# A fused attention and feed-forward kernel on one core: g's cast in batch index 1 from VectorE to ScalarE, the forms' steps over two slots, P's blocks of batch index 2 in pairs, and its score steps moved

## The chip, the cores and the metric

The kernel runs on one core of a Trainium2 chip. A core has a matrix engine (TensorE, PE in the profile; its weight loads are PEld), a vector engine (VectorE, DVE), an activation engine (ScalarE, ACT), GpSimd (POOL) and SyncE (SP), which here issues nearly all DMAs. Each engine runs its own instructions in the order in which they stand; semaphores order the engines among each other. The metric is the device time of one execution in microseconds, the median of several runs.

## The reference

Eight batches of eight heads: a slot attention (softmax over 32 memory slots, then over the scores) is followed by a feed-forward layer with SiLU. All is float32.

```python
def _attn_ref(q, k, v, phi):                 # q, k, v: 8 x 8 x 576 x 64; phi: 8 x 8 x 576 x 32
    a = np.exp(phi - np.max(phi, axis=2, keepdims=True))
    a = a / (np.sum(a, axis=2, keepdims=True) + 1e-09)
    k_m = np.einsum('bhsm,bhsd->bhmd', a, k)
    v_m = np.einsum('bhsm,bhsd->bhmd', a, v)
    scores = scale * np.matmul(q, k_m.transpose(0, 1, 3, 2))
    scores = scores - np.max(scores, axis=-1, keepdims=True)
    attn = np.exp(scores)
    attn = attn / (np.sum(attn, axis=-1, keepdims=True) + 1e-09)
    return np.matmul(attn, v_m)
def _moe_ref(x, w_in, w_out):                # x: 4608 x 512; w_in: 512 x 2048; w_out: 2048 x 512
    h = x @ w_in
    g = h * (1.0 / (1.0 + np.exp(-h)))
    return g @ w_out
```

## The kernel before

**What is multiplied.** The attention's last product and the first feed-forward product are taken together: per batch the kernel forms P = v_m · w_in (tiles `pm`), and h = attn · P. Every float32 factor is kept as a high part (a cast to fp32r, a copy) and a low part (the factor minus its high part), and a product is three matmuls: high·high, high·low, low·high. So each g = silu(h) needs a cast and a subtraction, and so do P (`p_split`: ACT casts at L677, DVE subtracts at L679) and the attention weights (`s_high` on ACT at L472, `s_low` on DVE at L479).

**Slots.** The work of a batch runs in 16 slots. Batch indices 0 and 1 take one block of 128 columns of the 2048 per slot. In a slot of batch index 1, PE does 12 matmuls for `h` (L701), then side work that a table of events puts there, then the 12 matmuls of `acc` (L746) for g of the slot before. In between ACT takes silu of h (L728, into `gbuf`; the 64 left-over columns into `gleft` at L730) and DVE casts g (L718) and takes the low part (L720), both into `gparts`, which holds two such pairs in turn. `h` is one PSUM tile, so the next h waits until ACT has read it. After slot 15 of an odd batch come four steps for the left-over tokens of two batches (`accleft` in batch index 1, `lsum` later; called steps 16 to 19 here, NFC = 16). From batch index 2 on, the second product is done with seven products in place of eight (`forms`, `st_step`, L854 and L893), whose weights `kept` and `saved` are derived from w_out by `w_forms` during batch index 1: eight pieces j, each with a step 0 (five DVE instructions, L814 to L821) and a step 1 (ACT casts at L835, DVE subtractions at L836, a DMA of 256 KB to `forms`).

**Side work for the next batch.** While batch b runs, the attention of batch b + 1 is made: `phi_max`, `phi_fold`, `phi_sub` (DVE), `phi_exp` (ACT), `e_mm` (PE, then DVE and ACT into `kvn`), `e_tr`, `s_all` (scores on PE, transposed by DVE), `s_max`, `s_sub` (L426, L430, DVE), `s_exp` (L434, ACT; the switch to the exponential's table and back is an ACT_TABLE_LOAD each), `s_sum` (L438 to L440), `s_norm` (L444), `s_back` (L464), `s_high`, `s_low`. P's four blocks of 512 columns (`p_mm`, L649) need w_in's blocks, which `win_load` brings back from HBM (1 MB each). `p_mm` with `beside` puts its result into two tiles of the pool `acc` (`pacc`), so that a second block need not wait for the tile `bg`.

**What sets the order.** `ev(b, slot, fn, ...)` enters a step into the table; the main loop runs the entries of a slot after that slot's h and silu. PE and ACT run in the order in which the code records their work. DVE's and SP's order is left to a scheduler, bounded by `behind(i, other)`, which puts an instruction after another on the same engine; `last_split[-1]` is the last subtraction of g's low part. In batch index 1 the scheduler is free to put `s_max` to `s_low` ahead of the slot's own split. POOL has nothing to do here.

Of the kernel before, what the change touches and what calls it, by code (L numbers as in the profile page):

```python
# [25 lines left out]
NFC = DFF // P  # L26
CW = 256
JW = 512
# [20 lines left out]
def attn_ffn_kernel(  # L49
# [756 lines left out]
    def w_forms(j, step):  # L806


        if step == 0:
            while len(kept) < 3 * j + 3:  # L810
                keep(*homes_left.pop(0))
            f = at[0]["forms", j] = sb.tile([P, 2, DMODEL], F32, tag="cva", name="wf", bufs=1)
            c = slice(2 * j, 2 * j + 2)
            i = nc.vector.tensor_tensor(f, as_f32(wo_hi[:, c]), as_f32(wo_lo[:, c]), op=ALU.add)  # L814
            if j == 0:
                behind(i.ins, last_split[-1])
            b11, b12, b21, b22 = (f[:, k, q * Q : (q + 1) * Q] for k in range(2) for q in range(2))
            nc.vector.tensor_tensor(b11, b12, b11, op=ALU.subtract)
            nc.vector.tensor_tensor(b12, b22, b12, op=ALU.add)
            nc.vector.tensor_tensor(b22, b22, b11, op=ALU.add)  # L820
            nc.vector.tensor_tensor(b21, b22, b21, op=ALU.subtract)  # L821
            return
        f = at[0]["forms", j].rearrange("p k (q f) -> p (k q) f", q=2)
        t1 = sb.tile([P, 1, DMODEL], F32R, tag="cva1", name="t1", bufs=1)
        runs = [[t1, 0, 1]]
        for u in range(3 * j, 3 * j + 3):
            t, i = kept_at[u]
            if t is runs[-1][0]:
                runs[-1][2] = i + 1
            else:  # L830
                runs.append([t, i, i + 1])
        n = 0
        for t, i, e in runs:
            src, to = f[:, n : n + e - i], t[:, i:e]
            nc.scalar.activation(to[:, :, :Q], src, AF.Copy)  # L835
            nc.vector.tensor_tensor(to[:, :, Q:], src, to[:, :, :Q], op=ALU.subtract)  # L836
            n += e - i
        load(saved[j], as_f32(t1[:, 0]))
# [182 lines left out]
    def steady(b, n):  # L1021


        early = b > 2
        if not early:
            ev(b, 1, phi_max, n)
            for i in range(3):
                ev(b, 2, phi_fold, n, i)
            ev(b, 3, phi_sub, n)
        ex = exp_slots(b)[0]  # L1030
        em = ex + 1 + b % 2
        ev(b, ex, phi_exp, n)
        ev(b, em, e_mm, n)
        for hf in range(2):
            ev(b, em + 1, load_q, n, hf)
        ev(b, ex + 4, e_tr, n)
        ev(b, ex + 5, s_all, n)
        ev(b, 9 if early else 10, s_max, n, ALL)
        ev(b, 10, s_sub, n, ALL)
        ev(b, 11, s_exp, n, ALL)  # L1040
        ev(b, 12 if early else 11, s_sum, n, ALL)
        ev(b, 13 if early else 12, s_norm, n, FIRST)
        turn = NFC + 3 if b % 2 else 14 if early else 13
        ev(b, turn, s_back, n, FIRST)
        ev(b, turn, s_high, n, FIRST)
        ev(b, turn, s_low, n, FIRST)
        for k in range(3):
            ev(b, 10 + 2 * k, win_load, n, k)
        if b % 2:
            ev(b, NFC, win_load, n, 3)  # L1050
        for k in range(2):
            ev(b, NFC + 2 if b % 2 else 13 + k, p_mm, n, k * JW, JW, True, b % 2 and k)
        m = n + 1
        if m < B:
            ev(b, ex + 3, load_kv, m, range(2))
            ev(b, ex + 3, load_phi, m)
            ev(b, ex + 6, load_kv, m, range(2, FULLC))
            ev(b, 7 if early else 14, phi_max, m)
            for i in range(3):
                ev(*((b, 11 + i) if early else (b + i // 2, (14, 15, 0)[i])), phi_fold, m, i, load)  # L1060
            ev(b + 1, 1, phi_sub, m)

    for b in range(B):
        n = b + 1
        if b == 0:
            for j in range(2, DFF // CW):
                ev(b, 2 * j - 1.5, p_mm, b, j * CW, CW)
        elif b == 1:
            ev(b, 0, win_save)
            for j in range(1, NJ):  # L1070
                ev(b, 4 * j - 3, p_mm, b, j * JW, JW)
            for j in range(NP):
                ev(b, 1.5 * j + 2, w_forms, j, 0)
                ev(b, 1.5 * j + 2.5, w_forms, j, 1)
        else:
            pair = b > 2 and b % 2 == 0
            if not pair:
                ev(b, 0, win_load, b, 3)
            ev(b, 0 if b > 2 else 1, p_mm, b, 2 * JW, JW)
            if b > 2:  # L1080
                ev(b, 3, s_norm, b, SECOND)
                for fn in (s_back, s_high, s_low):
                    ev(b, 4 + b % 2, fn, b, SECOND)
            late = b % 2 and 2 < b < B - 1
            ev(b, 0 if pair else 4 if late else 2, p_mm, b, 3 * JW, JW, not late, pair)
            if n < B:
                steady(b, n)
            if late:
                ev(b, 4, p_rest, b, 3 * JW)
            continue  # L1090
        at_slot = (
            (4, 5, 6, 7.5, 9, 9.5, 11.5, 12.5, 13, 13.5, 14, 14) if b == 0
            else (1, 2, 3, 5, 9, 10, 10, 11, 12, 13, 13, 14)
        )
        mx, sub, ex, em, tr, s0, s1, sx, se, ss, sn, sk = at_slot
        ev(b, mx, phi_max, n)
        if n == 1:
            ev(b, sub, phi_allmax, n, (0, 1), (0,))
            ev(b, sub + 0.5, phi_allmax, n, (0, 1), (1,))
        else:  # L1100
            for i in range(3):
                ev(b, sub, phi_fold, n, i)
        ev(b, sub + 0.5, phi_sub, n)
        ev(b, ex, phi_exp, n)
        ev(b, em, e_mm, n)
        ev(b, 14 if b == 0 else em + 1, load_kv, n + 1, range(FULLC if b == 0 else 2))
        ev(b, tr, e_tr, n)
        ev(b, em, load_q, n, 1)
        if n == 1:
            ev(b, s0, s_mm, n, 0)  # L1110
            ev(b, s1, s_mm, n, 1)
        else:
            ev(b, s0, s_all, n)
        if b == 0:
            ev(b, s1, load_q, n + 1, 0)
        else:
            ev(b, s1 + 1, load_kv, n + 1, range(2, FULLC))
        ev(b, sx, s_max, n, ALL)
        ev(b, sx, s_sub, n, ALL)
        ev(b, se, s_exp, n, ALL)  # L1120
        ev(b, ss, s_sum, n, ALL)
        ev(b, sn, s_norm, n, ALL)
        for u in (FIRST, SECOND) if n == 1 else (ALL,):
            ev(b, sk, s_back, n, ALL, u)
            ev(b, sk, s_high, n, ALL, u)
        ev(b, sk, s_low, n, ALL)
        ev(b, sk, load_phi, n + 1)
        if b == 0:
            ev(b, 14, p_mm, n, 0, JW)
        else:  # L1130
            for k in range(3):
                ev(b, 12 if k == 2 else 6 + k, win_load, n, k)
            for k in range(2):
                ev(b, 12 + 2 * k, p_mm, n, k * JW, JW)
    slots = [1.5, 1.5] + [2 * j - 1 if k == "i" else min(2 * j - 0.5, 12.5) for k, i in later for j in [i - 1 if k == "i" else i]]
    to_do = list(slots)
    for slot in slots:
# [151 lines left out]
    for b in range(B):  # L1289
# [10 lines left out]
        for fc in range(NFC if b < 2 else 0):  # L1300
# [3 lines left out]
                        fn(*a)  # L1304
                continue
            h = ffn1(b, fc, low_last=b == 1 and fc == 0)
            gs = split(silu(b, fc, h))
            for part in range(2):
                if b == 0:
                    finish((2 * part, 2 * part + 1))  # L1310
                traced = nc.cur_bb.bb.instructions
                n = len(traced)
                late = set()
                for fn, a in events.pop((b, fc + part / 2), []):
                    m = len(nc.cur_bb.bb.instructions)
                    fn(*a)
                    if fn is phi_max:
                        late.update(i.name for i in list(nc.cur_bb.bb.instructions)[m:])
                if b == 0:
                    for i in list(nc.cur_bb.bb.instructions)[n:]:  # L1320
                        if i.engine == ACT:
                            behind(i, last_silu[-1])
                        elif i.engine == DVE and (fc > 10 or i.name in late):
                            behind(i, last_split[-1])
            if b:
                finish(range(NI))
            prev = ("main", b, fc, gs)
        if b % 2:
            for n in range(NLS):
                gs = left_split(b, n)  # L1330
                if b > 1:
                    run(b, NFC + n)
                finish((0, 1, 2, 3))
                prev = ("left", b, n, gs)
    finish((0,))
# [55 lines left out]
```

## Time and profile before

| | us |
|---|---|
| median of 3 runs | 678.78 (678.55 to 679.08) |
| the profiled execution | 678.47 |
| its span, first to last instruction | 676.7 |
| what lies around the span (678.47 - 676.7) | 1.8 |
| mean granted clock | 0.999 |

A stretch in the views runs from the start of one block of matmuls on PE to the start of the next: batch index 1 from 105.66 (h of slot 0) to 189.35 us, its left-over steps to 197.52, batch index 2 to 272.77. Matmuls of one engine overlap in the records, so a block's own length is read from start to start, not from its busy time. On DVE and ACT an instruction's start can lie a little ahead of the end of the one before it, as the instructions are pipelined. The page's longest groups of PE are h of batches 2 to 7 (L854, 168.7 us in 1152 matmuls) and the seven products (L893). The trace shows the matmuls of all stages at the full clock.

### The profile page before, as it was taken

The numbers are of one execution on the slowest core, as the hardware profiler recorded it, in microseconds if no ns is written. First come the engines' busy times: TensorE is split into PE (matmuls) and PEld (weight loads), VectorE is DVE, ScalarE is ACT, GpSimd is POOL, SyncE is SP. The second block draws the span as 40 slices with busy tenths as digits, with TensorE's granted clock in tenths as the row PEclk, the third lists the DMA queues.
The fourth block names the chain that finished last, engine by engine and source line by source line (L and its number), as shares of the span: only waits on it lengthen the run. The fifth ranks groups of instructions, "written<-read, shape, count | busy, mean of one in ns | idle before, by whom it ended". The sixth has DMA issues, their size and how long they took to land.

```text
span 676.7 us, 14541 instructions
## 1 busy us (share of the span) xinstructions
PE 667.1 (99%) x5792; PEld 588.6 (87%) x5792; DVE 518.6 (77%) x1093; ACT 368.5 (54%) x681; POOL 0.7 (0%) x6
## 2 busy tenths in 40 slices
PE   7999999999999999999999999999999999999997
PEld 3577778787888998999988999899997999889996
DVE  4997899988948689868877688877877668867653
ACT  3878684533625556654655546564654546554541
POOL 0000000000000000000000000000000000000000
PEclk9999999999999999999999999999999999999999
DMA  9998975224270552253420535116430204300001
GB/s 340 373 339 276 315 304 192 81 103 146 78 233 22 184 183 100 79 180 124 179 95 16 185 97 179 70 42 237 157 126 32 86 2 156 111 31 17 32 1 47
DMA packets 37907, 93.92 MB, mean 139 GB/s; under 512 B 4688, under 2 KB 21456, under 8 KB 34256
## 3 DMA queue, kind: packets, MB, share of 16 engines
q1 hardware_dynamic: 36816, 90.22, 38.4%
q10 hardware_dynamic: 1024, 2.77, 1.1%
q8 instruction: 46, 0.75, 0.5%
q14 instruction: 21, 0.17, 0.1%
HBM read 77.22 MB, written 15.73 MB: 137 GB/s over the span
## 4 chain that ended last, share of the span: by engine, by line
PE 73%; DVE 10%; issue 2%; ACT 2%; DVEq 0%; ACTq 0%
PE sum L893 35%; PE h L854 22%; PE lsum L977 5%; PE bg L649 3%; PE acc L746 3%; PE h L701 2%; PE accleft L746 2%; DVE gparts L720 1%; PE bg L335 1%; PE bg L382 1%; DVE pm L679 1%; DVE kept L836 1%; DVE gparts L718 1%; DVE smx L426 1%; PE h L335 1%
## 5 line engine op out<-in xcount | busy, mean ns | idle before, releaser
L854 PE MATMUL h<-aparts,pm 128*128 128x288 f32 x1152 | 168.7, 295 | 0.0
L854 PEld LDWEIGHTS h<-aparts,pm 128*128 128x128 f32 x1152 | 157.3, 188 | 0.8
L868 ACT ACTIVATE gbuf<-h 128x512 f32<-128x512 f32 x96 | 57.3, 597 | 117.0 <-PE h L854 113.7
L893 PE MATMUL sum<-wo_hi,aparts 128*128 128x256 f32 x384 | 102.6, 289 | 0.0
L893 PE MATMUL sum<-kept,aparts 128*128 128x256 f32 x576 | 100.1, 282 | 0.0
L893 PE MATMUL sum<-wo_lo,aparts 128*128 128x256 f32 x384 | 100.0, 282 | 0.0
L873 DVE TENSOR_TENSOR gbuf<-gbuf 128x256 f32<-128x256 f32 x96 | 40.5, 422 | 71.4 <-ACT gbuf L868 70.9
L882 ACT ACTIVATE aparts<-gbuf 128x512 fp32r<-128x512 f32 x86 | 54.4, 633 | 63.4 <-DVE gbuf L877 63.4
L746 PE MATMUL acc<-wo_hi,gparts 128*128 128x512 f32 x256 | 85.0, 397 | 0.2
L893 PEld LDWEIGHTS sum<-wo_hi,aparts 128*128 128x128 f32 x384 | 72.8, 189 | 11.5 <-ACT gleft L870 10.1
L893 PEld LDWEIGHTS sum<-kept,aparts 128*128 128x128 f32 x576 | 82.6, 191 | 0.0
L884 DVE TENSOR_TENSOR gparts<-gbuf,aparts 128x512 fp32r<-128x512 f32 x86 | 59.5, 692 | 19.1 <-ACT aparts L882 19.1
L893 PE MATMUL sum<-wo_hi,gparts 128*128 128x256 f32 x384 | 73.2, 281 | 0.0
L893 PEld LDWEIGHTS sum<-wo_lo,aparts 128*128 128x128 f32 x384 | 73.1, 190 | 0.0
L893 PE MATMUL sum<-kept,gparts 128*128 128x256 f32 x288 | 65.5, 282 | 0.0
L746 PEld LDWEIGHTS acc<-wo_hi,gparts 128*128 128x128 f32 x256 | 47.6, 188 | 14.5 <-DVE gparts L720 1.5
L893 PEld LDWEIGHTS sum<-wo_hi,gparts 128*128 128x128 f32 x384 | 59.4, 190 | 0.0
L701 PEld LDWEIGHTS h<-aparts,pm 128*128 128x128 f32 x372 | 51.7, 188 | 6.8 <-issue 3.4
L701 PE MATMUL h<-aparts,pm 128*128 128x288 f32 x372 | 56.0, 299 | 0.6 <-DVE aparts L612 0.5
L872 ACT ACTIVATE aparts<-gbuf 128x384 fp32r<-128x384 f32 x96 | 50.4, 525 | 0.0
L746 PE MATMUL acc<-wo_lo,gparts 128*128 128x512 f32 x128 | 49.3, 393 | 0.4 <-DVE wo_lo L182 0.4
L893 PEld LDWEIGHTS sum<-kept,gparts 128*128 128x128 f32 x288 | 47.9, 190 | 0.0
(225 smaller groups left out, 956.1 us busy)
## 6 DMA issues: line engine op xcount, KB each, us to landing
win<-win_saved SPq DMA_DIRECT2D x24, 1024.0 KB, 5.2
kv<-in_kv SPq DMA_DIRECT2D x28, 516.0 KB, 5.0
q<-in_q SPq DMA_DIRECT2D x16, 576.0 KB, 6.2
raw<-in_w_in SPq DMA_DIRECT2D x14, 512.0 KB, 7.6
raw<-in_w_out SPq DMA_DIRECT2D x6, 1024.0 KB, 6.5
win_saved<-win SPq DMA_DIRECT2D x4, 1024.0 KB, 8.6
phi<-in_phi SPq DMA_DIRECT2D x7, 576.0 KB, 8.3
out<-oo SPq DMA_DIRECT2D x26, 128.0 KB, 2.3
```

The costliest lines, as they stand in the source:

```text
L335: nc.tensor.matmul(pt[p][M * r : M * (r + 1), :KVW], e[:, p, c, M * r : M * (r + 1)], kvt[c][:, p, r], start=c == 0, stop=False, skip_grou ...
L649: nc.tensor.matmul((bg[p][M * r : M * (r + 1)] if beside else bg[M * r : M * (r + 1), p, :w]).rearrange("p (k f) -> p k f", f=P), kvT[D * ...
L701: nc.tensor.matmul(h[:, hf, :HALF], wt[:, p, fs], a[:, p, hf * HALF : (hf + 1) * HALF], start=n[hf] == 0, stop=n[hf] == 5, skip_group_chec ...
L746: nc.tensor.matmul(acc[key], gt[:, cs], wt[:, fc], start=fc == 0 and n == 0, stop=fc == NFC - 1 and n == 2)
L854: nc.tensor.matmul(h[:, i, :HALF], wt[:, p, f : f + P], a[:, p], start=n == 0, stop=n == 5)
L868: nc.scalar.activation(gbuf[:, :MAIN].rearrange("p (i f) -> p i f", i=2), h[:, :, :w], AF.Silu)
L872: nc.scalar.activation(hi[:, :3], g[:, 1:4], AF.Copy)
L873: nc.vector.tensor_tensor(g[:, 4:6], g[:, :1].broadcast_to([P, 2, P]), g[:, 1:3], op=ALU.subtract)
L882: nc.scalar.activation(hi[:, 3:], g[:, 4:], AF.Copy)
L884: last_split.append(nc.vector.tensor_tensor(lo[:, 3:], g[:, 4:], hi[:, 3:], op=ALU.subtract))
L893: nc.tensor.matmul(sums[bank][:, place * Q : (place + 1) * Q], gt[:, k], wt, start=bank not in begun, stop=True, skip_group_check=True,)
L977: nc.tensor.matmul(sums[k], part[gt][:, 2 * i + k], wt[:, fc], start=n == 0 and i == 0 and m == 0, stop=True, skip_group_check=True,)
```

## The change

It has two parts. In batch index 1, g is cast by ACT (L716 in the new kernel, step 2 of `split`) in all slots but 3 and 12, those in which ACT takes an exponential; so is the last slot of batch index 0. The forms' pieces get a table of slots, with a step 1 about two slots behind step 0 or less; pieces 1 and 2 are held behind a split and behind the subtraction into `kvn`. `phi_max` and the score steps on DVE are held behind the split of their slot. The first two blocks of P for batch index 2 go from slots 12 and 14 into step 18, the second beside the first; w_in's fourth block is loaded in step 16. In batch index 2, P's third and fourth block go into slot 0 as a pair, `e_tr` from slot 8 to 7, `s_all` from 9 to 8, `s_max` from 10 to 9, `s_norm` from 12 to 13, `s_back` to `s_low` from 13 to 14, P's first block for the next batch from 13 to 12, `phi_max` from 14 to 12, and the folds of the maxima from slots 14, 15 and 0 into 13, 14 and 15. Lines below L1033 shift by up to 6 in the new kernel.

```diff
@@ w_forms
-            if j == 0:
-                behind(i.ins, last_split[-1])
+            if j < 3:
+                behind(i.ins, last_kvn[0] if j == 2 else last_split[-1])
@@ steady(b, n)
-        ev(b, ex + 4, e_tr, n)
-        ev(b, ex + 5, s_all, n)
-        ev(b, 9 if early else 10, s_max, n, ALL)
+        ev(b, ex + 4 - (not early), e_tr, n)
+        ev(b, ex + 5 - (not early), s_all, n)
+        ev(b, 9, s_max, n, ALL)
...
-        ev(b, 13 if early else 12, s_norm, n, FIRST)
-        turn = NFC + 3 if b % 2 else 14 if early else 13
+        ev(b, 13, s_norm, n, FIRST)
+        turn = NFC + 3 if b % 2 else 14
...
-            ev(b, NFC + 2 if b % 2 else 13 + k, p_mm, n, k * JW, JW, True, b % 2 and k)
+            ev(b, NFC + 2 if b % 2 else (13 if early else 12 + k) + k, p_mm, n, k * JW, JW, True, b % 2 and k)
...
-            ev(b, 7 if early else 14, phi_max, m)
+            ev(b, 7 if early else 12, phi_max, m)
             for i in range(3):
-                ev(*((b, 11 + i) if early else (b + i // 2, (14, 15, 0)[i])), phi_fold, m, i, load)
+                ev(b, 11 + i if early else 13 + i, phi_fold, m, i, load)
@@ the table
+    FORM_SLOTS = (2, 4), (4, 5), (5.5, 6.5), (7, 8), (8.5, 9.5), (10, 11), (11.5, 13), (13, 14)
-            for j in range(NP):
-                ev(b, 1.5 * j + 2, w_forms, j, 0)
-                ev(b, 1.5 * j + 2.5, w_forms, j, 1)
+            for j, (slot, end) in enumerate(FORM_SLOTS):
+                if j:
+                    ev(b, FORM_SLOTS[j - 1][1], w_forms, j - 1, 1)
+                ev(b, slot, w_forms, j, 0)
+            ev(b, end, w_forms, j, 1)
         else:
-            pair = b > 2 and b % 2 == 0
+            pair = b % 2 == 0
             if not pair:
                 ev(b, 0, win_load, b, 3)
-            ev(b, 0 if b > 2 else 1, p_mm, b, 2 * JW, JW)
+            ev(b, 0, p_mm, b, 2 * JW, JW)
...
-            for k in range(3):
-                ev(b, 12 if k == 2 else 6 + k, win_load, n, k)
+            for k, slot in enumerate((6, 7, 12, NFC)):
+                ev(b, slot, win_load, n, k)
             for k in range(2):
-                ev(b, 12 + 2 * k, p_mm, n, k * JW, JW)
+                ev(b, NFC + 2, p_mm, n, k * JW, JW, True, k)
@@ the main loop
-            gs = split(silu(b, fc, h))
+            by_act = fc not in (3, 12) if b else fc == NFC - 1
+            gs = split(silu(b, fc, h), steps=(2, 1) if by_act else (0, 1))
...
-                    if fn is phi_max:
+                    if fn is phi_max or b and fn in (s_max, s_sub, s_sum, s_norm, s_back, s_low):
                         late.update(i.name for i in list(nc.cur_bb.bb.instructions)[m:])
...
+                for i in list(nc.cur_bb.bb.instructions)[n:] if b else ():
+                    if i.engine == DVE and i.name in late:
+                        behind(i, last_split[-1])
...
             for n in range(NLS):
                 gs = left_split(b, n)
-                if b > 1:
-                    run(b, NFC + n)
+                run(b, NFC + n)
```

Where the instructions go, at three places. First ACT in slots 13 to 15 of batch index 1, from the first form cast of a piece (`t`) on. Before:

```order
L835 ACTIVATE t_1861<-wf 128x256
L835 ACTIVATE kept<-wf 128x3x256
L728 ACTIVATE gbuf<-h 128x512
L730 ACTIVATE gleft<-h 128x64
L472 ACTIVATE aparts<-aT_1901 128x1152
L677 ACTIVATE pm<-bg 128x1024
L728 ACTIVATE gbuf<-h 128x512
```

and now:

```order
L728 ACTIVATE gbuf<-h 128x512
L730 ACTIVATE gleft<-h 128x64
L716 ACTIVATE gparts<-gbuf 128x512
L835 ACTIVATE t_1883<-wf 128x256
L835 ACTIVATE kept<-wf 128x3x256
L472 ACTIVATE aparts<-aT_1889 128x1152
L728 ACTIVATE gbuf<-h 128x512
L730 ACTIVATE gleft<-h 128x64
L716 ACTIVATE gparts<-gbuf 128x512
```

The last piece's casts stood in slot 13 and now stand in slot 14; `s_high` (L472) stands in slot 14 in both, ahead of the silu of slot 15, and the cast of P behind it is gone. Each silu is now followed by its cast.

Second DVE, in slots 13 to 15 of batch index 1. Before, from `s_sum` to the split of slot 15:

```order
L440 RECIPROCAL ssm<-ssm 128x36
L821 TENSOR_TENSOR wf<-wf 128x256
L444 TENSOR_TENSOR sc_1701<-sc_1701,ssm 128x1152
L718 CAST gparts<-gbuf 128x512
L836 TENSOR_TENSOR t_1861<-wf,t_1861 128x256
L720 TENSOR_TENSOR gparts<-gbuf,gparts 128x512
L836 TENSOR_TENSOR kept<-wf,kept 128x3x256
L464 STREAM_TRANSPOSE aT_1901<-sc_1701 128x576
L718 CAST gparts<-gbuf 128x512
L464 STREAM_TRANSPOSE aT_1901<-sc_1701 128x576
L720 TENSOR_TENSOR gparts<-gbuf,gparts 128x512
L479 TENSOR_TENSOR aparts<-aT_1901,aparts 128x1152
```

and now, from the split of slot 14 to that of slot 15:

```order
L720 TENSOR_TENSOR gparts<-gbuf,gparts 128x512
L818 TENSOR_TENSOR wf<-wf 128x256
L440 RECIPROCAL ssm<-ssm 128x36
L819 TENSOR_TENSOR wf<-wf 128x256
L444 TENSOR_TENSOR sc_1693<-sc_1693,ssm 128x1152
L820 TENSOR_TENSOR wf<-wf 128x256
L836 TENSOR_TENSOR t_1883<-wf,t_1883 128x256
L821 TENSOR_TENSOR wf<-wf 128x256
L464 STREAM_TRANSPOSE aT_1889<-sc_1693 128x576 x2
L836 TENSOR_TENSOR kept<-wf,kept 128x3x256
L718 CAST gparts<-gleft 128x512
L479 TENSOR_TENSOR aparts<-aT_1889,aparts 128x1152
```

(the next row is L720, the split of slot 15). `s_norm` (L444) stood ahead of the split of slot 14 and stands behind it now; the transposes (L464) stand behind all of the last form; and the first left-over cast (L718 from `gleft`) and `s_low` (L479) stand ahead of the split of slot 15.

Third PE, in the left-over steps 17 and 18, now (three more alternations of the two `pacc` tiles follow):

```order
L746 MATMUL accleft<-wo_lo,gparts 128x512
L746 MATMUL accleft<-wo_hi,gparts 128x512
L649 MATMUL bg<-win_0_1513,kvT_1644 32x512 x8
L649 MATMUL pacc_1997<-win_1_1558,kvT_1644 32x512
L649 MATMUL pacc_1998<-win_1_1558,kvT_1644 32x512
```

Before, the two blocks (one each in slots 12 and 14) stood between a slot's h and its acc; this is slot 14 in the difference:

```order
 L746 MATMUL acc_1250<-wo_hi,gparts 128x512
 L701 MATMUL h<-aparts,pm 128x288 x12
-L649 MATMUL bg<-win_1_1564,kvT_1652 32x512 x8
 L746 MATMUL acc_1238<-wo_hi,gparts 128x512
 L746 MATMUL acc_1238<-wo_lo,gparts 128x512
```

So 16 matmuls a block left the slots, and 32 came in between the first and the second group of `accleft`.

## The prediction

> **What bounds the kernel now.** I read the page's head first, then the busy time by stage, from start to start of PE's blocks (columns: stretch, length, then busy us and instructions of PE, PEld, DVE, ACT, POOL, the granted clock, DMA share and GB/s).
>
> ```profile
> span 676.7 us, 14541 instructions
> PE 667.1 (99%) x5792; PEld 588.6 (87%) x5792; DVE 518.6 (77%) x1093; ACT 368.5 (54%) x681; POOL 0.7 (0%) x6
> ```
>
> ```profile
> 105.66:189.35 83.69, 83.35 (x607) 67.30 (x607) 74.36 (x146) 38.63 (x74) 0.00 (x0) 1.00 0.37 132
> 189.35:197.52 8.17, 8.17 (x37) 6.76 (x36) 2.21 (x4) 0.72 (x2) 0.00 (x0) 1.00 0.83 274
> 197.52:272.77 75.25, 75.12 (x715) 69.03 (x713) 58.27 (x133) 40.51 (x77) 0.00 (x0) 1.00 0.38 124
> 357.61:432.00 74.39, 74.39 (x715) 69.07 (x714) 57.50 (x130) 41.27 (x80) 0.00 (x0) 1.00 0.34 114
> ```
>
> PE sets the time everywhere. In batch index 1 (first row) DVE is nearly as full, 74.36 of 83.69 us; ACT has 38.63. So what the change can win are PE's waits there, and what it can lose is a DVE chain that comes late. PE's waits in this batch, from the view of waits between 100 and 200 us (total, times, longest), and five groups of `acc` from start to start:
>
> ```profile
> PEld acc L746 <- DVE gparts L720: 1.5, 3, 0.5
> ...
> PEld h L701 <- DVE kvn L361: 0.5, 1, 0.5
> ```
>
> ```profile
> 107.35:110.50 3.15, 3.08 (x12) 2.01 (x12) 1.70 (x3) 1.00 0.20 74
> 126.33:129.47 3.14, 3.04 (x12) 1.99 (x12) 0.00 (x0) 1.00 0.00 0
> 134.44:137.57 3.13, 3.02 (x12) 2.18 (x12) 0.00 (x0) 1.00 0.92 342
> 173.63:176.38 2.75, 2.75 (x12) 2.07 (x12) 0.00 (x0) 1.00 0.03 6
> 183.53:189.35 5.82, 5.75 (x24) 4.24 (x24) 1.67 (x3) 1.00 0.77 277
> ```
>
> Twelve undisturbed matmuls take 2.75 us (fourth row). The first two rows lose 0.40 and 0.39 to a late g; the third loses 0.26 (side work ahead of a group costs 0.12 by itself, below) to `kvn`; the last, two groups, 0.32. That is 1.4 us, all that waits could give in batch index 1.
>
> **P's blocks.** The rows are h, a block of P, acc and the next h around slot 12, and a pair in batch index 4:
>
> ```profile
> 166.47:168.15 1.68, 1.68 (x13) 1.51 (x11) 1.68 (x3) 0.00 (x0) 0.00 (x0) 1.00 0.85 346
> 168.15:169.17 1.02, 1.02 (x17) 0.18 (x16) 1.02 (x3) 0.25 (x1) 0.00 (x0) 1.00 0.07 24
> 169.17:172.04 2.87, 2.87 (x20) 2.36 (x13) 2.51 (x6) 2.84 (x6) 0.00 (x0) 1.00 0.25 97
> 172.04:173.63 1.59, 1.59 (x14) 1.58 (x12) 1.59 (x4) 1.59 (x2) 0.00 (x0) 1.00 0.00 0
> 359.28:361.16 1.88, 1.88 (x33) 0.49 (x33) 1.07 (x4) 1.18 (x4) 0.00 (x0) 1.00 0.04 9
> ```
>
> A single block costs 1.02, and 0.09 and 0.12 at its edges (1.68 against 1.59, 2.87 against 2.75): 1.23. A pair costs 1.88 and the same edges: 2.09. So slots 12 and 14 lose **-2.46**, step 18 gains **+2.09**. Batch index 2 gains 0.37 by its pair; its stretch is also 0.86 longer than batch 4's, which has this arrangement already, so between -0.37 and -0.86, and I take **-0.6**.
>
> **The cast.** DVE loses 14 casts of batch index 1 and one of batch 0, 0.42 each (a row below). ACT's cast of g is not in this stage; the nearest row is the same copy out of `gbuf` in later batches:
>
> ```profile
> L882 ACT ACTIVATE aparts<-gbuf 128x512 fp32r<-128x512 f32 x86 | 54.4, 633 | 63.4 <-DVE gbuf L877 63.4
> ```
>
> 0.63, with 0.42 (were it as fast as DVE) as the other end; ACT's spare 45 us hide it as long as nothing long stands ahead of it. The waits at 107.35 and 126.33 go: the cast no longer queues on DVE behind `s_low` or a form's sum, **-0.79**. What is late next at 134.44 is `kvn`. PE would be there at 137.57 - 0.26 - 0.79 = 136.5. In slot 5, h ends at 129.47 + 1.68 - 0.79 = 130.4; 0.16 of hand-over, silu 0.60 and cast 0.63 make 131.8. DVE then has the split (0.60), seven rows of 0.34 to 1.14 up to the last `kept` (0.34, 0.34, 1.14, four times 0.34) and four tiny ones for `rs` (0.4): 136.0. The rows below give 0.7 of waiting for ACT's half of `kvn` and 0.35: 137.1. PE waits 0.6 where it waited 0.26, **+0.34**. At slot 11 the gain is 0.45.
>
> ```profile
> L361 DVE TENSOR_SCALAR kvn<-h,rs 128x128 f32<-128x128 f32 x1 | 0.4, 351 | 0.7 <-ACT kvn L359 0.7
> ```
>
> **The end of batch index 1** decides. The rows of DVE and ACT in slots 12 to 15 of before (start, duration):
>
> ```profile
> 170.19 0.42 DVE L836 TENSOR_TENSOR kept<-wf,kept 128x256 fp32r<-128x256 f32 x1
> 170.53 0.42 DVE L718 CAST gparts<-gbuf 128x512 fp32r<-128x512 f32 x1
> 170.86 1.22 DVE L814 TENSOR_TENSOR wf<-wo_hi,wo_lo 128x1024 f32<-128x1024 f32 x1
> 172.00 0.69 DVE L720 TENSOR_TENSOR gparts<-gbuf,gparts 128x512 fp32r<-128x512 f32 x1
> 172.60 0.42 DVE L818 TENSOR_TENSOR wf<-wf 128x256 f32<-128x256 f32 x1
> 172.97 1.35 DVE L438 TENSOR_REDUCE ssm<-sc 128x36 f32<-128x1152 f32 x1
> 174.24 1.22 DVE L679 TENSOR_TENSOR pm<-bg,pm 128x1024 fp32r<-128x1024 f32 x1
> ```
>
> ```profile
> L464 DVE STREAM_TRANSPOSE aT<-sc 128x576 f32<-128x576 f32 x2 | 1.5, 770 | 0.0
> ```
>
> ```profile
> 170.47 1.28 ACT L434 ACT_TABLE_LOAD   x1
> 171.77 1.17 ACT L434 ACTIVATE sc<-sc 128x1152 f32<-128x1152 f32 x1
> 172.84 1.01 ACT L677 ACTIVATE pm<-bg 128x1024 fp32r<-128x1024 f32 x1
> 173.87 1.28 ACT L728 ACT_TABLE_LOAD   x1
> 175.17 0.60 ACT L728 ACTIVATE gbuf<-h 128x512 f32<-128x512 f32 x1
> ...
> 178.22 0.60 ACT L728 ACTIVATE gbuf<-h 128x512 f32<-128x512 f32 x1 [0.53 <-PE h L701]
> ...
> 181.94 1.17 ACT L472 ACTIVATE aparts<-aT 128x1152 fp32r<-128x1152 f32 x1 [3.00 <-DVE aT L464]
> ```
>
> From start to start DVE takes 0.34 for 256 wide, 0.60 for a split, 1.14 for 1024 and 1.27 for 1152 wide (the rows overlap by some 0.08). A silu follows its h by 0.16 (h of slot 14 from 176.38, 1.68 long; silu at 178.22). In the new order, counted from T, the end of slot 11's h (163.73 - 0.45 = 163.3):
>
> - Cast 11 is done at T + 1.4. DVE: split 0.6, a form's three subtractions 1.3, L426 1.27, L814 1.14, L430 1.35, done at T + 7.1.
> - ACT, whose table is already switched: exponential 1.17, table back 1.3, silu 13 0.6, cast 0.63: T + 10.9.
> - Only then may DVE do split 13, and `s_sum` is held behind it: 0.6, three subtractions 1.3, L438 1.27, L814 1.14, L439 and L440 0.45, split 14 0.6, six rows of 0.34, L444 1.27 and the two transposes 1.5: 10.1, of which two short rows overlap more; I take 9.8. Transposes done at T + 20.7. Before, they were done at 181.9, T + 18.2 on that kernel's clock.
> - ACT: L472 1.17, and only behind it silu 15 0.6 and cast 15 0.63: T + 23.1. Slot 15's h has been ready since T + 17.4 (four slots of 4.34).
> - PE wants cast 15 at T + 17.4 + 2.75 = T + 20.1 and waits **3.0**. DVE has L479 (1.36) between L472 and split 15 (0.69), so the low part comes at T + 24.0, 0.4 after PE needs it. 3.4 in place of 0.32 is **+3.1**.
>
> So the two blocks of P that left slots 12 and 14 had filled PE while DVE caught up; without them PE is early and waits. The size is bounded: a chain without any overlap of rows is 1.3 longer (+4.4). From below there is a second lock: the left-over cast ahead of L479 writes the `gparts` half that PE reads until T + 20.1, and with 0.42, 1.27 and 0.69 behind that, the low part of slot 15 cannot come before T + 22.5, where T + 20.6 is wanted. That leaves 1.9, or +1.6; below it, only if DVE's order ran otherwise than it stands.
>
> [...]
>
> **Other edits.** Behind ACT's silus nothing new waits but what is named. On SP, w_in's fourth load now stands ahead of the last form's store and phi of batch 3; the store frees the buffer for the third output tile, but PE needs that tile's bank only after another 2.75 us, so zero, at most 0.5. In batch index 2 the folds' seven small DMAs go out in slots 13 to 14, behind a 1 MB load; DVE's L296 waits for them, and slot 15's forms queue behind it: between 0 and 0.5, taken as zero, as batch 4 has the same order and is the shorter stretch.
>
> **The sum.** -0.79 + 0.34 - 2.46 + 3.1 + 2.09 - 0.6 = +1.7. The profiled execution is 676.7 of span and 1.8 around it, 678.47; 680.15. It lies 0.31 under the median of the runs, so **680.4**.
>
> **The rivals.** (0.2%, or 1.36 us, is about what a measurement of this kernel can tell from no change.)
> - The forecast, the late transposes: 679.7 to 681.5. Chance 0.58, of which some three tenths fall within 0.2%.
> - Only the second lock binds, since DVE's chain ends 1.5 us earlier (an exponential released sooner would do it): +0.2, 679.0. Chance 0.24. Against it: from T + 10.9 on DVE has no gap to give.
> - **Faster:** the wait in slot 15 doesn't arise, because DVE, relieved of 14 times 0.34 = 4.8 us, is ahead there. The point is whether the transposes end by T + 17.6; then the sum is -0.79 + 0.34 - 2.46 - 0.32 + 2.09 - 0.6 = -1.7, 677.0. For it: DVE's busy share falls. Against it: it idles early (split 1 waits for a cast) and the hold behind split 13 leaves the score steps to the end. Chance 0.09.
> - A longer loss: no overlap of rows on DVE, 681.8, chance 0.05; or PE's clock gives way after its wait. If the 12 matmuls behind it ran at half speed, that is 2.75 more: 683.2. Every stretch above shows a clock of 1.00, but no wait quoted here is over 0.5. Chance 0.04. [...]
>
> Faster: 0.09. Within 0.2%: 0.24 and 0.17 of the forecast's own, 0.41. Slower: 0.50. The range runs from the second lock less the unknown of the other terms, 678.0, to 682.0; it leaves out the faster case and most of the last.
>
> **What would show it.** Right: in the new trace slot 15's silu stands behind L472 and ends some 5 us after its h; a gap of about 3 us ahead of the last `acc` group; the waits at 107 and 126 us gone; batch index 2 about 74.6 long. Wrong: the transposes done before slot 15's h, a gap under 2 us, or a new wait in batch index 2 at L296 or at the score matmuls, now one slot sooner behind their loads.

## The result, and the profile after

| | before | after |
|---|---|---|
| median of 6 runs | 678.85 (678.55 to 679.08) | 682.26 (681.84 to 682.88) |
| ratio, 95% interval | | 1.0051 [1.0038, 1.0064] |
| the profiled execution | 678.47 | 682.88 |
| its span | 676.7 | 681.1 |
| mean granted clock | 0.999 | 0.997 |

The kernel got slower by 3.4 us, where 1.6 had been forecast (680.4 against 678.78). The profiled execution of after is the slowest of its six; 1.01 us of its distance lies ahead of batch index 1, whose first h starts at 106.67 in place of 105.66. So 107.35 of before is 108.34 here.

The first thing to read is the clock. Below is the line PEclk of the page of after; one of its 40 slices, at 187 to 204 us, is not full.

```profile
PEclk9999999999989999999999999999999999999999
```

Next come, from the view of TensorE's waits from 100 to 200 us (us in total, times, longest), the lines that bear on the prediction's terms:

```profile
PEld acc L746 <- ACT gparts L716: 3.6, 1, 3.6
PEld acc L746 <- issue: 1.0, 2, 0.8
PEld h L701 <- DVE kvn L361: 1.0, 1, 1.0
...
PEld acc L746 <- DVE gparts L720: 0.6, 1, 0.6
```

The three waits for a low part in slots 0, 4 and 15 (1.5 together) have become one of 0.6; the new wait of 3.6 is for ACT's cast of g in slot 15; the one for `kvn` is twice as long. The stretches at the places of the prediction's terms, in the columns of the view of windows (us from start to start, busy time and count of PE, PEld, DVE, ACT and POOL, granted clock, DMA share, GB/s):

```profile
108.34:111.08 2.74, 2.74 (x14) 2.26 (x13) 0.82 (x2) 2.54 (x6) 0.00 (x0) 1.00 0.11 36
126.90:129.66 2.76, 2.76 (x15) 2.25 (x14) 0.23 (x1) 2.50 (x5) 0.00 (x0) 1.00 0.00 0
134.63:138.24 3.61, 3.02 (x20) 2.17 (x13) 3.58 (x12) 1.22 (x3) 0.00 (x0) 1.00 0.90 337
181.68:192.24 10.56, 7.22 (x27) 5.20 (x25) 8.69 (x15) 4.95 (x8) 0.00 (x0) 0.88 0.65 230
...
189.46:192.87 3.41, 3.41 (x10) 2.69 (x9) 1.49 (x4) 1.72 (x4) 0.00 (x0) 0.53 0.48 178
...
195.49:197.36 1.87, 1.87 (x33) 0.48 (x32) 1.00 (x2) 0.68 (x1) 0.00 (x0) 1.00 0.77 246
```

The first two stretches lose nothing any more, the third loses 0.86 over 2.75. Slot 15's two `acc` groups take 10.56 where before took 5.82, and within them the granted clock is 0.88; the fifth row is a stretch of full PE work at about half clock. The timeline of PE shows the order of the two:

```profile
184.19 0.39 PE L746 MATMUL acc<-wo_hi,gparts 128*128 128x512 f32 x1
187.80 0.50 PE L746 MATMUL acc<-wo_hi,gparts 128*128 128x512 f32 x1 [3.22 <-ACT gparts L716]
...
189.22 0.40 PE L746 MATMUL acc<-wo_lo,gparts 128*128 128x512 f32 x1
189.46 0.85 PE L746 MATMUL acc<-wo_hi,gparts 128*128 128x512 f32 x2
190.10 0.63 PE L746 MATMUL acc<-wo_lo,gparts 128*128 128x512 f32 x1
```

PE idles for 3.22 us and goes on at full speed (a matmul is recorded with 0.40) for 1.7 us; only then does a matmul take 0.63, until about 193 (the view of windows has the granted clock at 1.00 from 187.80 to 189.46 and at 0.50 from 189.68 to 193.09). So the loss has two parts: a wait, and matmuls at half clock that begin after PE is busy again.

What made the wait is read on ACT, slots 13 to 15:

```profile
171.50 1.17 ACT L434 ACTIVATE sc<-sc 128x1152 f32<-128x1152 f32 x1 [0.61 <-DVE sc L430]
173.25 1.28 ACT L728 ACT_TABLE_LOAD   x1 [0.59 <-PE h L701]
174.55 0.60 ACT L728 ACTIVATE gbuf<-h 128x512 f32<-128x512 f32 x1
...
175.18 0.63 ACT L716 ACTIVATE gparts<-gbuf 128x512 fp32r<-128x512 f32 x1
...
184.09 0.84 ACT L835 ACTIVATE kept<-wf 128x768 fp32r<-128x768 f32 x1 [2.42 <-DVE wf L821]
185.44 1.16 ACT L472 ACTIVATE aparts<-aT 128x1152 fp32r<-128x1152 f32 x1 [0.50 <-DVE aT L464]
186.51 0.58 ACT L728 ACTIVATE gbuf<-h 128x512 f32<-128x512 f32 x1
186.99 0.22 ACT L730 ACTIVATE gleft<-h 128x64 f32<-128x64 f32 x1
187.12 0.63 ACT L716 ACTIVATE gparts<-gbuf 128x512 fp32r<-128x512 f32 x1
```

Slot 15's h has been ready since 181.7; its silu starts at 186.51, the instant `s_high` lets ACT go, and `s_high` waited for the transposes. DVE, behind split 13, has no gap up to them:

```profile
175.84 0.69 DVE L720 TENSOR_TENSOR gparts<-gbuf,gparts 128x512 fp32r<-128x512 f32 x1 [1.97 <-ACT gparts L716]
...
177.72 1.35 DVE L438 TENSOR_REDUCE ssm<-sc 128x36 f32<-128x1152 f32 x1
...
181.71 1.34 DVE L444 TENSOR_TENSOR sc<-sc,ssm 128x1152 f32<-128x1152 f32 x1
...
183.98 1.43 DVE L464 STREAM_TRANSPOSE aT<-sc 128x576 f32<-128x576 f32 x2
...
186.17 0.41 DVE L718 CAST gparts<-gleft 128x512 fp32r<-128x512 f32 x1
186.63 1.36 DVE L479 TENSOR_TENSOR aparts<-aT,aparts 128x1152 fp32r<-128x1152 f32 x1
187.91 0.68 DVE L720 TENSOR_TENSOR gparts<-gbuf,gparts 128x512 fp32r<-128x512 f32 x1
```

### The profile page after: what moved, and what is told of

It is laid out like the page before. It is cut to its first block, busy times and chain, and to the rows that moved or that the text cites. A ratio compares the mean times of both kernels' runs of the same rounds, so it can differ in the third digit from the quotient of the medians.

```text
span 681.1 us, 14525 instructions
## 1 busy us (share of the span) xinstructions
PE 666.7 (98%) x5792; PEld 589.5 (87%) x5792; DVE 512.4 (75%) x1080; ACT 376.9 (55%) x698; POOL 0.7 (0%) x6
## 4 chain that ended last, share of the span: by engine, by line
PE 86%; DVE 3%; ACT 1%; issue 1%; DVEq 0%; ACTq 0%
PE sum L893 36%; PE h L854 22%; PE acc L746 9%; PE h L701 5%; PE lsum L977 5%; PE bg L649 3%; PE accleft L746 2%; PE bg L335 1%; PE bg L382 1%; PE pacc L649 1%; PE h L335 1%; ACT L728 0%; DVE gparts L720 0%; DVE kept L836 0%; PE bg L345 0%
```

## The experiments

Theory A: the hold of the score steps behind split 13 and the place of `s_high` ahead of silu 15 make PE wait, and that wait is what takes the clock down. (T, in the expectations and below, is the end of slot 11's h, as in the prediction.) Each kernel is an edit of the changed one unless it says otherwise; times stand against the kernel before on the same chip, which had a median of 678.8 to 679.0 in each series.

### Is it the idle time that halves the clock?

Dummy matmuls ahead of slot 15's second `acc` group (`n_dummy` is 14 in one kernel and 5 in the other):

```diff
                 run(b, NFC + n)
+                if b == 1 and n == 0:
+                    keep_warm(bgtile()[:, 0], n_dummy)
                 finish((0, 1, 2, 3))
```

> The changed kernel with 14 dummy matmuls of about 0.22 us (3.1 us in all, results unused) on PE in the left-over step 16, where PE waits 3.4 us for the cast of slot 15; nothing else is changed. Theory A (PE's idle time there makes the clock fall to a half for 3.41 us): PE waits for the cast as before but is not idle, no half clock in slot 15's acc, 682.3 - 1.7 = 680.6 us (680.2 to 681.0). Rival B (the matmuls behind the wait are slow for another reason, such as ACT and DVE working on the same tiles beside them): the matmuls of 0.63 us stay and the time is 682.3 us or up to 0.3 more.

Measured: 680.62 us, ratio 1.0024 [1.0015, 1.0033], mean clock 0.999 to 1.000 in all ten executions. The wait for the cast is as long in time as before, but PE is busy in it:

```profile
180.71:190.08 9.37, 9.07 (x41) 5.63 (x39) 8.52 (x15) 4.83 (x8) 0.00 (x0) 1.00 0.64 219
```

9.37 in place of 10.56, at a clock of 1.00. PE idles for 0.18 us there. More work on PE made the kernel 1.6 us faster; rival B falls.

> The changed kernel with 5 of the same dummy matmuls (1.1 us) at the same place: PE idles about 2.2 us in one piece in place of 3.3. Theory A with a least idle time between 2.2 and 3.3 us: no half clock, 680.6 us as with 14 dummies. Theory A with a least idle time under 2.2 us: the half clock stays, 682.3 us. Rival B: 682.3 us.

Measured: 680.96 us, 1.0034 [1.0022, 1.0047]. PE idled 2.14 us in the profiled execution, clock full. But of the six executions four had a mean clock of 0.999 and 680.75 to 681.00 us, and two one of 0.997 and 681.79 and 682.09 us. So neither branch of the expectation holds: in this kernel, with 2.14 us of idle time in the profile, the clock was lower in two of six executions and full in four.

### What holds the cast back?

The hold taken off:

```diff
-                    if fn is phi_max or b and fn in (s_max, s_sub, s_sum, s_norm, s_back, s_low):
+                    if fn is phi_max:
```

> The changed kernel without the new hold of the score steps on DVE behind their slot's split (phi_max stays held as in the kernel before); ACT's order is the same, DVE's changes: s_sub, s_sum, s_norm and one transpose stand ahead of splits 12 and 13 again. Theory A (the hold behind split 13, that is behind exponential, silu 13 and cast 13, makes the transposes late): transposes done before T+17, s_high waits only for the last form's casts, cast 15 done about T+20.3, low part T+21.1: PE waits under 1 us in place of 3.9, no half clock, 682.3 - 1.7 - 2.8 = 677.8 us (677.2 to 678.6). Rival E (the hold is not it: the cast's place on ACT behind s_high and the last form's casts is enough): the wait stays over 2.5 us, 680 us and more.

Measured: 678.71 us, 0.9994 [0.9984, 1.0003]: the whole loss against before is gone, though the time is 0.1 over the expected range. The timeline of DVE in this kernel:

```profile
173.79 1.36 DVE L444 TENSOR_TENSOR sc<-sc,ssm 128x1152 f32<-128x1152 f32 x1
175.18 0.78 DVE L464 STREAM_TRANSPOSE aT<-sc 128x576 f32<-128x576 f32 x1
175.88 0.65 DVE L720 TENSOR_TENSOR gparts<-gbuf,gparts 128x512 fp32r<-128x512 f32 x1
...
177.72 0.77 DVE L464 STREAM_TRANSPOSE aT<-sc 128x576 f32<-128x576 f32 x1
```

The transposes end at 178.49, 14.5 after T (here 164.01), where the changed kernel has T + 21.1. The two groups take 7.29 at full clock, and PE idles 1.13 for the cast: that rest is the last form's step 1, still ahead of silu 15 with `s_high`, and is why the expected "under 1 us" was missed.

`s_high` behind the cast of slot 15, first alone, then with the left-over cast held back as well, and the latter alone:

```diff
-            else (1, 2, 3, 5, 9, 10, 10, 11, 12, 13, 13, 14)
+            else (1, 2, 3, 5, 9, 10, 10, 11, 12, 13, 13, 15)
```

```diff
+                m, other = len(nc.cur_bb.bb.instructions), last_split[-1]
                 gs = left_split(b, n)
+                if b == 1 and n == 0:
+                    for i in list(nc.cur_bb.bb.instructions)[m:]:
+                        if i.engine == DVE:
+                            behind(i, other)
```

> The changed kernel with s_back, s_high and s_low of batch index 1 entered in slot 15 in place of 14, the left-over cast left where it is: s_high then stands behind the cast of slot 15 on ACT, and the left-over cast, its subtraction and the last form's subtraction ahead of split 15 on DVE. Theory A with the prediction's second lock (the left-over cast waits for PE's read until T+20.1): high part about T+21.2, low part about T+23, so acc is late by some 2.5 us in place of 3.7, half clock gone or short: 682.3 - 1.7 - 1.2 = 679.4 us (679.0 to 680.4). Without the second lock it would be that of the kernel with the left-over cast held back as well, 680.0 us less what its later eviction cost there (0.5), 679.5: the two differ in the trace, by the wait for the low part (1.5 against 0.2 us), rather than in the time.

Measured: 680.49 us, 1.0023 [1.0014, 1.0033], 0.1 over the expected range; six executions at 0.999 to 1.000 with 680.14 to 680.56, four at 0.997 with 680.72 to 681.18. PE idles 1.56 for the cast, then 0.61 for the low part. The second lock is there now: the left-over cast waits for PE's read.

```profile
183.90 0.43 DVE L718 CAST gparts<-gleft 128x512 fp32r<-128x512 f32 x1 [0.33 <-PE acc L746]
```

> The changed kernel with batch index 1's s_back, s_high and s_low entered into slot 15 in place of 14 (so the silu and the cast of slot 15 stand ahead of s_high on ACT) and with the left-over cast held behind the split of slot 15. Theory A: the cast of slot 15 then waits only for the last form's casts on ACT and is done about T+21.3 (T: end of slot 11's h), the low part at T+22.1, so PE waits 1.2 to 2.0 us in place of 3.9 and the clock stays full: 682.3 - 1.7 - 2.2 = 678.4 us (677.8 to 679.0). Rival B (slow matmuls not caused by the idle time): 680.1 us. Rival C (transposes and s_high are not what the cast waits for): the wait stays over 3 us and the time at 682 us.

Measured: 680.00 us, 1.0013 [1.0004, 1.0022], 1.6 over what was expected. PE idles 1.56 for the cast; half of the ten executions have a clock of 0.997 and a median of 680.23, the others one of 679.42. And a new wait stands behind it:

```profile
188.90 0.50 PE L746 MATMUL accleft<-wo_hi,gparts 128*128 128x512 f32 x1 [0.46 <-ACT oo L760]
```

The output's eviction (L760), which frees the bank of the left-over group, now queues behind `s_high` and the transposes. Moving `s_high` without making it earlier only moves the wait on.

> The changed kernel with only the left-over cast held behind the split of slot 15 on DVE. Theory A: in the changed kernel that cast ran 0.4 us ahead of s_low while s_low waited for s_high, so it costs nothing; high part and low part of slot 15 come as before: 682.3 us (681.9 to 682.6), half clock there. Rival (the second lock binds): split 15 comes 0.4 us or more sooner, 681.8 us or less.

Measured: 681.48 us (680.60 to 682.77), 1.0039 [1.0026, 1.0052]. The median is lower than expected, and by itself it would speak for the rival; but the trace shows the same wait of 3.22, and split 15 starts 23.57 after T in both kernels, so the left-over cast costs nothing in the changed kernel. One of the seven executions had a clock of 0.999, and it is the one of 680.60; why the others, at 0.995 to 0.997, spread more than the changed kernel's is not settled.

### The parts of the change

P's first two blocks back in slots 12 and 14:

```diff
             for k in range(2):
-                ev(b, NFC + 2, p_mm, n, k * JW, JW, True, k)
+                ev(b, 12 + 2 * k, p_mm, n, k * JW, JW)
```

> The changed kernel with P's first two blocks for batch index 2 back in slots 12 and 14, one each, as in the kernel before. The prediction's terms for them are -2.46 (out of the slots) and +2.09 (pair in step 18), the latter 1.87 by the profile of the changed kernel. Theory A: the block in slot 12 moves PE and the chain of ACT and DVE alike, the block in slot 14 moves PE alone, so PE's wait for the cast shrinks from 3.9 by about 1.2 to 2.7 us and the half clock goes: 682.3 + 2.46 - 1.87 - 1.2 - 1.7 = 680.0 us; with the half clock still there 681.7. Rival D (the blocks had filled all of the time for which PE now waits): the wait shrinks by 2.4 and more, 678.8 us.

Measured: 683.45 us by three executions, 1.0064 [1.0047, 1.0081]; a fourth took 2647.01 us, nothing on record says why, and it is left out. That is over all that was expected. PE still idles 2.91 us for the cast, since the second block brings its own cast onto ACT, ahead of silu 15:

```profile
186.98 1.01 ACT L677 ACTIVATE pm<-bg 128x1024 fp32r<-128x1024 f32 x1
187.88 0.59 ACT L728 ACTIVATE gbuf<-h 128x512 f32<-128x512 f32 x1
```

And the clock is lower for longer, by the windows 0.73 over slot 15's two groups, that is 2 x 0.27 x 11.32 = 6.1 us at half clock (twice the missing share of the clock, times the length) where the changed kernel has 2 x 0.12 x 10.56 = 2.5 there and the rest of its 3.4 in the left-over group:

```profile
183.37:194.69 11.32, 8.41 (x27) 6.04 (x26) 8.59 (x15) 5.87 (x9) 0.00 (x0) 0.73 0.61 214
```

So the blocks had not filled PE for the chain; most of the wait is there with them.

```diff
-            by_act = fc not in (3, 12) if b else fc == NFC - 1
+            by_act = not b and fc == NFC - 1
```

> The changed kernel with all casts of g in batch index 1 on DVE again (batch 0's last stays on ACT); forms' table and holds stay. Theory A: the two waits of 0.4 us at the acc groups of slots 0 and 4 come back (+0.8), the silu of slot 15 still stands behind s_high and the late transposes, and the cast then queues on DVE behind s_low, so PE's wait is as long as before or 0.5 longer and the half clock stays: 683.0 us (682.4 to 683.8). Rival F (the cast on ACT is what makes slot 15 late, by 0.63 at the end and by 0.63 ahead of split 13): the wait is 1.2 shorter, the half clock may go, 681.8 us or 680.1 us.

Measured: 684.12 us, 1.0075 [1.0061, 1.0089], above the range. PE idles 1.23 for the low part of slot 14 and 3.25 for the cast of slot 15, with the half clock behind (a granted clock of 0.75 over the 13.05 us of slot 15's two groups). In the changed kernel the cast's move to ACT is worth 1.8 us (684.12 - 682.28), waits and clock together; it is not what makes slot 15 late.

The kernel before with batch index 2's part alone (the diff's lines on `steady`, the pair in slot 0 and the load in step 16):

> The kernel before with the change's part on batch index 2 alone (P's last two blocks as a pair in slot 0, e_tr and s_all one slot earlier, norm and back one later, P's first block for the next batch in slot 12, folds in 13 to 15, w_in's fourth block loaded in step 16); batch index 1 keeps its casts, its forms and its single blocks of P. Prediction's term: -0.6, between -0.37 and -0.86. The changed kernel's stretch of batch index 2 was 0.87 shorter than before's. Expected: 678.9 - 0.87 = 678.0 us (677.8 to 678.4). Rival: part of the 0.87 comes from batch index 1's part (P's first blocks made in step 18 and cast there), then 678.4 to 678.9.

Measured: 677.82 us, 0.9979 [0.9970, 0.9988], 1.0 to 1.2 under the kernel before (the medians of all its series and of its own). The profile has 0.87 of it: the stretch is 74.38 long in this kernel as in the changed one.

The second form's step 1 half a slot later:

```diff
-    FORM_SLOTS = (2, 4), (4, 5), (5.5, 6.5),
+    FORM_SLOTS = (2, 4), (4, 5.5), (5.5, 6.5),
```

> The changed kernel with the second form's step 1 entered at 5.5 in place of 5, which puts its ACT casts and DVE subtractions behind the halves of kvn in slot 5. Theory A: PE's wait of 1.0 us (0.74 beyond the side work's own edge) for kvn at slot 6 falls to 0.3 or less and all later work is as much sooner: 682.3 - 0.7 = 681.6 us (681.3 to 681.9). Rival (the wait in slot 15 absorbs it, since ACT's and DVE's chain does not move with PE): 682.3 us.

Measured: 681.31 us, 1.0037 [1.0026, 1.0048]. The wait for `kvn` falls from 1.0 to 0.3. This kernel also gives the cleanest look at the clock. Its profiled execution had the same wait and no half clock; the row of the wait on PE, and the view of windows of slot 15's two groups and of the second alone:

```profile
186.84 0.50 PE L746 MATMUL acc<-wo_hi,gparts 128*128 128x512 f32 x1 [3.23 <-ACT gparts L716]
...
180.71:190.09 9.38, 6.04 (x27) 4.35 (x26) 8.53 (x15) 4.84 (x9) 0.00 (x0) 1.00 0.64 219
186.84:190.09 3.25, 3.14 (x13) 2.29 (x14) 2.46 (x6) 1.68 (x3) 0.00 (x0) 1.00 0.48 184
```

It took 680.26 us; the seven others, at a clock of 0.995 to 0.997, took 681.03 to 682.29.

> The changed kernel once more, unchanged, in more executions. Theory A': whether the clock halves after a wait of 3.2 us is not fixed by the wait alone (the kernel with the second form at 5.5 showed the same wait of 3.23 us at full clock in its profiled execution, 680.26 us, and seven others at a mean clock of 0.995 to 0.997, 681.0 to 682.3 us): most executions at a clock of 0.997 and 682.2 us, the odd one at 0.999 or 1.000 and then about 1.0 to 1.7 us shorter. Rival: the mean clock and the time are not related within one kernel.

Measured: 682.28 us, 1.0055 [1.0041, 1.0069]; all five at a clock of 0.994 to 0.997. With the first series that is eleven of eleven, so the odd one without a half clock did not come, and the relation of clock and time within one kernel rests on form55, warm5, turn15 and free15.

| kernel | longest idle of PE in slot 15 (profiled run), us | executions at a clock of 0.997 or less |
|---|---|---|
| best2 (below) | none | 0 of 5 |
| warm14 | 0.18 | 0 of 10 |
| no_hold | 1.13 | 0 of 10 |
| turn15, free15 | 1.56 | 9 of 20 |
| warm5 | 2.14 | 2 of 6 |
| blocks_back | 2.91 | 3 of 3 |
| after (both series), left_held, form55 | 3.22 | 24 of 26 |
| dve_cast | 3.25 | 4 of 4 |

An execution's mean clock doesn't say where in the kernel the clock was lost; only a profile does. The kernel before, which has no such wait, also has a mean clock of 0.997 in 2 of the 71 executions whose clock is on record with these experiments (679.64 and 681.19 us), so single counts in the table can have another place.

### A version that beats both

no_hold, free15 and form55 together, and the last form's step 1 in slot 15 too:

```diff
-    FORM_SLOTS = ... (4, 5), ... (13, 14)
+    FORM_SLOTS = ... (4, 5.5), ... (13, 15)
```

> The changed kernel with five edits: the score steps not held behind the splits, s_back to s_low entered in slot 15, the last form's step 1 entered in slot 15, the left-over cast held behind the split of slot 15, and the second form's step 1 entered at 5.5 in place of 5 (so that kvn's halves stand ahead of it on ACT and DVE). Theory A: PE waits neither for kvn (-0.7) nor more than 0.3 us in slot 15, no half clock: 682.3 - 1.7 - 3.5 - 0.7 = 676.4 us (675.9 to 677.2), faster than both. Rival G (what is taken out of slot 15 comes late in step 16 or 17, where s_high and s_low stand ahead of the output's evictions and the left-over splits): 677.5 to 679 us, with a wait at accleft.

Measured: 676.33 us (676.15 to 677.03), 0.9963 [0.9950, 0.9975], as theory A had it. ACT takes silu and cast of slot 15 first, at 180.58, with nothing ahead of them:

```profile
180.58 0.60 ACT L728 ACTIVATE gbuf<-h 128x512 f32<-128x512 f32 x1 [3.07 <-PE h L701]
181.08 0.22 ACT L730 ACTIVATE gleft<-h 128x64 f32<-128x64 f32 x1
181.21 0.64 ACT L716 ACTIVATE gparts<-gbuf 128x512 fp32r<-128x512 f32 x1
...
182.79 1.16 ACT L472 ACTIVATE aparts<-aT 128x1152 fp32r<-128x1152 f32 x1
```

```profile
180.38:186.11 5.73, 5.63 (x26) 4.35 (x25) 5.11 (x10) 4.50 (x9) 0.00 (x0) 1.00 0.67 250
186.11:189.33 3.22, 3.22 (x12) 2.07 (x13) 1.81 (x4) 1.15 (x2) 0.00 (x0) 1.00 0.73 264
```

The second fence is the view of windows: slot 15's two groups take 5.73, and the left-over group 3.22, 0.4 more than the 2.81 it takes in no_hold; so much of rival G is true.

## Why the prediction was right and wrong

**Right: the wait and its chain.** Counted from T (164.34 in the profile of after), the forecast and the trace: L430 done T + 7.1 and 7.1; cast 13 done 10.9 and 11.5; transposes done 20.7 and 21.1; cast 15 done 23.1 and 23.4; low part 24.0 and 24.2; PE ready for it 20.1 and 20.1. The largest slip is at the cast of slot 13, 0.59 at the table load: the forecast let it run straight behind the exponential, but it stands behind the wait for slot 13's h. Without the half clock (form55) the two groups take 9.38, that is 3.88 over two undisturbed ones, where 3.4 was forecast; 3.38 of it is the wait for the cast, the rest the low part and the restart. no_hold showed that the hold behind split 13 carries more than half of it (9.38 down to 7.29), and best2 that nearly all of the rest goes with what stands ahead of silu 15 on ACT and with the left-over cast on DVE (down to 5.73).

**The failing step: the clock rival.** "PE's clock gives way after its wait" stood at a chance of 0.04 and outside the sum. It happened in all eleven executions of the changed kernel, by their mean clock of 0.994 to 0.997. Its size, forecast at 2.75 by 12 matmuls at half speed, is 1.6: warm14, which has the same chain and next to no idle time, is at 680.62, against 682.26. Without it 680.62 - 678.91 = 1.71 is left, the sum that was forecast; that the two agree so closely is luck, as the other terms, below, are off by up to 0.5 in both directions. Nearly all of the error in the time, 682.3 against 680.4, is this term (0.06 of it is a slip of the sum itself: 680.15 + 0.31 is 680.46). What failed in the reasoning was to take "no wait quoted here is over 0.5" as evidence about a wait six times as long: no run on record then had shown such a wait, so the 0.04 was no more than the author's estimate. In the runs the half clock came after 3.22 us of idle time in the profile of the changed kernel, and after 1.56 and 0.61 us in that of turn15.

**The other terms.** First two waits: -0.79 forecast, -0.41 and -0.38 measured. `kvn`: +0.34 forecast, 3.61 - 3.13 = +0.48 measured; form55 confirms the place. Blocks out of the slots: the stretches of slots 12 and 14 are 1.59 and 2.75 as forecast, -2.46. Pair in step 18: +2.09 forecast, measured 1.87 and 0.22 at its edges (2.81 and 5.58 in form55's rest of the left-over steps against 8.17 for all three groups in before). Batch index 2: -0.6 forecast, -0.87 measured, the upper bound given; part2 shows it to belong to that part alone. By the terms: 1.7 as forecast + 0.5 (wait) + 0.1 (`kvn`) - 0.3 (batch index 2) + 1.6 (half clock) = 3.6, against 3.4 by the medians.

**A sentence that falls:** "the two blocks of P that left slots 12 and 14 had filled PE while DVE caught up". With them back PE still idles 2.91 us, because they bring casts and subtractions to the same chain. What kept the kernel before from that wait, to judge by no_hold, was that its score steps could run ahead of the splits.

**The second lock** does not bind in the changed kernel (left_held). Once `s_high` is out of the way it does: in turn15 the left-over cast waits for PE until T + 20.05, where 20.1 was forecast, and PE idles 0.61 for the low part; in free15 it doesn't idle for it.

## What to carry to other kernels

A wait on TensorE cost twice in the changed kernel: its own 3.22 us, and matmuls at half clock behind it (1.6 us against warm14). A lower clock came with waits of 1.56 us and more, in some executions or all, and in none of the 25 executions of no_hold, warm14 and best2, with 1.13 us and less. Price both, or fill the wait with work that isn't needed. Holding side work behind the main work's splits protects each split but can put a whole chain at the end of the stage: follow the held steps to the instruction that the last split waits for. When one step of a table is moved, move what stands with it on the in-order engine (here `s_high`, the last form's casts and the hold) together: each alone left another wait.

## What the runs showed of the hardware

In the changed kernel the half clock began after TensorE had work again: the wait ends at 187.80, and the first slow matmuls are in the row from 189.46. It lasted 3.41 us there (granted clock 0.50 from 189.68 to 193.09). In blocks_back and dve_cast the first matmul behind the wait, at 189.18 and 188.73, is slow already: it is recorded with 0.80 and 0.79, where form55 at full clock has 0.50. By the granted clock over slot 15's two groups, 0.73 of 11.32 us and 0.75 of 13.05, these kernels spent about 6.1 and 6.5 us of them at half clock.

Whether the half clock comes is not set by the length of the wait alone: the profile of form55 shows 3.23 us of idle time without it, that of the changed kernel 3.22 us with it, and in the kernels with 1.56 us 9 of 20 executions had a mean clock of 0.997. What else decides stays open. By the medians of one kernel's executions with and without it, the half clock costs 0.8 us (free15, turn15) to 1.2 us (form55, where one execution is without), and 1.6 between the changed kernel and warm14.
